# A planned attention and two gated MLPs on one core: planner costs from a trace, the words' guard offered to GpSimd, later weights let in at set points

## The chip, the cores and the metric

The kernel runs on one core of a Trainium2 chip. The metric is the device time of one execution in microseconds (us). The kernel before took 1058.9 us (median of 3 runs, 1057.39 to 1060.78).

## The reference

```python
# attention: 4 batches, 8 heads, 576 positions, 64 columns a head, all float32
scores = where(mask, scale * q @ k.T, -1e9)     # heads 0-3: a window of 32; heads 4-7: 32 steps of 4 back
attn   = softmax(scores);  o = attn @ v
x = o laid out as 2304 tokens x 512
# first gated MLP, d_ff 1536
xn = x / sqrt(mean(x * x) + 1e-6) * rms_g
x  = (silu(xn @ w_gate) * (xn @ w_val)) @ w_out
# second gated MLP, d_ff 1536
y  = (sigmoid(x @ w_gate2) * (x @ w_val2)) @ w_out2
```

The MLP weights arrive in 8-byte floating point and are read as pairs of 32-bit words.

## The kernel before

**Products.** Every operand of an MLP product is split into a high and a low part (`split`: the high part is a cast on ScalarE, the low part a subtraction on GpSimd; VectorE may do either), and a product is three matmuls: high by high, high by low, low by high.

**Stages.** Attention works in 48 groups of three blocks of 64 queries (`attn_group`): scores on TensorE (L709), mask and row maximum on VectorE (L720), exponential on ScalarE (L726), the sum's reciprocal on VectorE (L733, L734), normalisation on GpSimd (L739), transposes on TensorE (L751), values on TensorE (L763). When the groups of a chunk of 384 tokens are done, `x_norm` makes that chunk's operand: squares on ScalarE (L807), sums on GpSimd (L815) and TensorE (L823), a Newton iteration (twelve small GpSimd operations, L857 to L861), a copy `rb` on VectorE (L864), its transposes on TensorE (L879), a scaling on VectorE (L891, tile `xn`, two buffers) and a split into `xo`. The transposes of `rb`, the scores and the transposes of the groups share a ring of two PSUM banks, `att`.

The first MLP runs in two passes over d_ff, each with 6 chunks of tokens by 6 blocks of 128 rows of d_ff: 72 steps. A step is a gate product `g`, a value product `v` (both L982) and an output product `y` (L1019), 12 matmuls each for g, v and y; between them stand tanh on ScalarE (L994), two multiplications on VectorE (L996, L1000) and the split of `h`. The steps of the first pass begin while attention still runs, and the groups stand between them on TensorE. The second MLP has three passes; its gate and value products are block products with fewer multiplications (`unit`, L1160), whose sums are added on VectorE (L1176), gated (L1186, L1192) and split into `h`. It needs sums and differences of the weights (L496 on VectorE, L499 on GpSimd) and of its input (L935, L938).

**Weights.** `words` turns the 64-bit weights into float32: a square on ScalarE (L395), a guard on VectorE that zeroes what is too small (L401, one input, 128 x 512), and three VectorE operations that put the bits together (L404, L407, L410, two inputs each). The 18 weight tiles of the first pass are split at once; the 18 of the second pass and the 36 of the second MLP are stored to HBM and loaded again when they are due.

**Order.** The whole order is written by a planner (`Line.emit`). Every operation is added with its engines, a cost in us, a due time and its reads and writes. The planner keeps a clock for each engine, picks the operation that can start first, and emits it; so the costs and due times decide the order in which instructions stand in each engine's queue. An operation with `other=` may go to a second engine; a number of `PARAMS` is added to that engine's start as a penalty. `release` holds an operation back until the planner's clock has come so far. On the chip each engine runs its queue in order and waits for semaphores.

Of the kernel before, what the change touches and what calls it, by code (L numbers as in the profile page):

```python
# [8 lines left out]
F32 = mybir.dt.float32  # L9
F32R = mybir.dt.float32r  # L10
# [16 lines left out]
    "h_hi": 0.3, "h_lo": 0.5, "qk": 0.2, "norm": 4.0, "pts": 4.0, "o": 2.0, "snap": 150.0, "h_ahead": 50.0, "h2_ahead": 50.0, "evac": 150.0, "ys": 1.0,  # L27
    "ts": 1.0, "cross": 0.25, "same": 0.064, "dma_lat": 2.0, "dma_rate": 260e3,
# [171 lines left out]
def attention_then_two_gated_mlps(  # L200
# [26 lines left out]
    ONE, TWO = 2, 3  # L227
    NF1 = DF // P // ONE
# [138 lines left out]
    def words(p, f, i, load_due, due, release=0.0):  # L367
# [22 lines left out]
        def low():  # L390
# [79 lines left out]
    def weight_load(p, f, i, due):  # L470
        key = (layer_of(p), f, i)
        z = new("mid", "zm", [P, CW], F32, 3 * NF1) if p == 1 else one_of(Z_HOMES, [P, CW], F32)
# [4 lines left out]
    def weight_late(p, f, i, due):  # L477
        z = weight_load(p, f, i, due - 6 - 40 * (p == 1))
# [180 lines left out]
    def attn_load(b, hp, due):  # L659
# [33 lines left out]
    def attn_group(b, hp, g, due, banks, start):  # L693
# [55 lines left out]
        def turn():  # L749
# [50 lines left out]
    def x_norm(c, due, banks):  # L800
# [226 lines left out]
    def y_first(p, c, m, due):  # L1027
# [21 lines left out]
        if m < KD - 1:  # L1049
            return  # L1050
# [365 lines left out]
```

## Time and profile before

| | |
|---|---|
| median of three runs | 1058.9 us |
| the profiled execution: its own time | 1064.26 us |
| the profiled execution: its span | 1062.3 us |
| TensorE busy | 1001.8 us (94%) |
| VectorE, ScalarE, GpSimd busy | 692.7, 461.1, 524.4 us |
| HBM read, written | 103.55, 47.19 MB |

The span goes from the first to the last instruction; the execution's own time is 2.0 us more. Busy time says how long an engine had an instruction under way, blocked time in the instruction included, and not whether the end depended on it. PE is TensorE, DVE VectorE, ACT ScalarE, POOL GpSimd.

### The profile page before, as it was taken

The page shows a single profiled execution, that of the slowest core. Times are in us where ns is not written, and L with a number is a line of the kernel's source. Part 1 is how long each engine was busy: PE and PEld are TensorE (multiplying, and loading weights), DVE is VectorE, ACT ScalarE, POOL GpSimd, SP SyncE. Part 2 cuts the span into 40 slices and gives each one's busy share as a digit, 9 for nine tenths or more (in the row PEclk, how much of TensorE's full clock was granted, in tenths as well). Part 3 has the DMA queues.
Part 4 walks back from the last instruction along what each step waited for, and adds up shares of the span by engine and source line. Part 5 has one row for each costly group of instructions (what it writes and reads, how often), then busy time and mean ns, then how long its engine had stood idle before and what let it go on. Part 6 is the DMA issues. An engine that isn't in the chain of part 4 may idle for free.

```text
span 1062.3 us, 19957 instructions
## 1 busy us (share of the span) xinstructions
PE 1001.8 (94%) x7222; PEld 966.2 (91%) x7222; DVE 692.7 (65%) x1443; ACT 461.1 (43%) x1251; POOL 524.4 (49%) x671
## 2 busy tenths in 40 slices
PE   4978869999999999999999999999999999999997
PEld 3767758888899999999999989999999999999996
DVE  2689787876664697766656575658556675465633
ACT  2967545655532443222222354445554354444321
POOL 2557765555552585112223683538655385444411
PEclk7769879999999999999999999999999998999999
DMA  9648746867349466765672331204231333235234
GB/s 189 130 112 182 171 134 156 206 154 223 106 150 346 158 219 212 275 221 179 199 248 72 97 114 45 89 24 131 81 137 63 134 110 107 97 100 125 54 82 90
DMA packets 192978, 152.04 MB, mean 143 GB/s; under 512 B 135760, under 2 KB 164432, under 8 KB 192880
## 3 DMA queue, kind: packets, MB, share of 16 engines
q1 hardware_dynamic: 185896, 149.00, 47.8%
q10 hardware_dynamic: 6984, 1.77, 1.0%
q8 instruction: 57, 0.93, 0.4%
q14 instruction: 41, 0.34, 0.1%
HBM read 103.55 MB, written 47.19 MB: 142 GB/s over the span
## 4 chain that ended last, share of the span: by engine, by line
PE 75%; DVE 9%; DMA 5%; POOL 3%; issue 3%; ACT 3%; SPq 2%; ACTq 0%; DVEq 0%; POOLq 0%
PE y L1019 23%; PE g L982 12%; PE v L982 11%; PE att L1160 10%; PE g L1160 7%; PE v L1160 7%; PE att L709 2%; DVE wz L401 1%; ACT pr L726 1%; DMA wst<-in_moe_w_val_dram 1%; POOL pr L739 1%; DMA v<-in_v_dram 1%; DVE wz L404 1%; PE att L763 1%; SPq L621 1%
## 5 line engine op out<-in xcount | busy, mean ns | idle before, releaser
L1019 PE MATMUL y<-h,wo 128*128 128x288 f32 (+1 forms) x2016 | 371.6, 314 | 1.1 <-POOL h L421 1.1
L1019 PEld LDWEIGHTS y<-h,wo 128*128 128x128 f32 x2016 | 319.5, 189 | 3.7 <-POOL h L421 1.3
L421 POOL TENSOR_TENSOR h<-t,h 128x288 fp32r<-128x288 f32 (+1 forms) x157 | 160.4, 1024 | 282.5 <-ACT h L417 231.4
L982 PE MATMUL g<-xo,w 128*128 128x384 f32 x864 | 169.1, 344 | 4.1 <-ACT w L417 1.7
L982 PE MATMUL v<-xo,w 128*128 128x384 f32 x864 | 163.5, 337 | 0.0
L982 PEld LDWEIGHTS g<-xo,w 128*128 128x128 f32 x864 | 154.7, 193 | 6.3 <-ACT w L417 1.9
L982 PEld LDWEIGHTS v<-xo,w 128*128 128x128 f32 x864 | 150.1, 188 | 1.3 <-issue 0.2
L417 ACT CAST h<-t 128x288 fp32r<-128x288 f32 (+1 forms) x144 | 67.3, 471 | 151.8 <-DVE t L1000 99.8
L1176 DVE TENSOR_TENSOR t<-t,att 128x288 f32<-128x288 f32 x96 | 43.1, 449 | 79.0 <-PE att L1160 78.5
L994 ACT ACTIVATE t<-g 128x384 f32<-128x384 f32 x72 | 35.4, 492 | 132.4 <-PE g L982 132.3
L1160 PE MATMUL att<-xo,w 128*128 128x288 f32 x576 | 92.5, 296 | 0.0
L739 POOL TENSOR_SCALAR pr<-pr,rs 128x96 f32<-128x96 f32 x144 | 63.4, 456 | 49.2 <-DVE rs L734 29.4
L996 DVE SCALAR_TENSOR_TENSOR t<-t,g 128x384 f32<-128x384 f32 x72 | 39.7, 551 | 73.2 <-ACT t L994 73.0
L1160 PEld LDWEIGHTS att<-xo,w 128*128 128x128 f32 x576 | 82.0, 189 | 0.0
L421 POOL TENSOR_TENSOR xo<-xq,xo 128x576 fp32r<-128x576 f32 x35 | 52.8, 1516 | 35.2 <-ACT xo L417 32.8
L1160 PE MATMUL v<-xo,w 128*128 128x288 f32 x396 | 64.6, 299 | 3.1 <-DVE t L1176 2.9
L401 DVE TENSOR_SCALAR wz<-wz 128x512 f32<-128x512 f32 x72 | 48.7, 678 | 27.1 <-ACT wz L395 25.7
L1160 PE MATMUL g<-xo,w 128*128 128x288 f32 x396 | 64.7, 300 | 0.0
L407 DVE SCALAR_TENSOR_TENSOR wz<-wst,wz 128x512 int32<-128x512 int32 x72 | 63.2, 877 | 1.0
L410 DVE SCALAR_TENSOR_TENSOR wz<-wst,wz 128x512 int32<-128x512 int32 x72 | 61.3, 853 | 1.2
L404 DVE SCALAR_TENSOR_TENSOR wz<-wst,wz 128x512 int32<-128x512 int32 x72 | 60.8, 845 | 1.1
L726 ACT ACTIVATE pr<-pr,nmx 128x96 f32<-128x96 f32 x144 | 52.5, 369 | 18.8 <-DVE nmx L720 18.6
(166 smaller groups left out, 1587.7 us busy)
## 6 DMA issues: line engine op xcount, KB each, us to landing
z<-wz SPq DMA_DIRECT2D x54, 256.0 KB, 2.2
wst<-in_moe_w_gate_dram SPq DMA_DIRECT2D x24, 512.0 KB, 3.9
wst<-in_moe_w_val_dram SPq DMA_DIRECT2D x24, 512.0 KB, 5.7
wst<-in_moe_w_out_dram SPq DMA_DIRECT2D x24, 512.0 KB, 4.2
xq<-y SPq DMA_DIRECT2D x20, 576.0 KB, 5.4
x<-xo SPq DMA_DIRECT2D x12, 768.0 KB, 4.7
xo<-x SPq DMA_DIRECT2D x12, 768.0 KB, 6.3
z<-z SPq DMA_DIRECT2D x36, 256.0 KB, 2.8
```

What stands on the lines that cost most here:

```text
L401: add("DVE", 0.65, lambda: nc.vector.tensor_scalar(out=z.t.bitcast(F32), in0=z.t.bitcast(F32), scalar1=LEAST * LEAST, scalar2=MANTISSA, op ...
L404: add("DVE", 0.9, lambda: nc.vector.scalar_tensor_tensor(out=z.t, in0=top(), scalar=3, in1=z.t, op0=ALU.logical_shift_left, op1=ALU.bitwis ...
L407: add("DVE", 0.9, lambda: nc.vector.scalar_tensor_tensor(out=z.t, in0=top(), scalar=-0x40000000, in1=z.t, op0=ALU.bitwise_and, op1=ALU.bit ...
L410: add("DVE", 0.9, lambda: nc.vector.scalar_tensor_tensor(out=z.t, in0=low(), scalar=29, in1=z.t, op0=ALU.logical_shift_right, op1=ALU.bitw ...
L417: add("ACT", act(n), lambda: nc.scalar.copy(out=hi(), in_=src()), reads=reads, writes=[key] + [order] * bool(order), tiles=tiles + [dst], ...
L421: add("PL", pool(n), lambda: nc.gpsimd.tensor_tensor(out=lo(), in0=src(), in1=hi().bitcast(F32), op=ALU.subtract), reads=reads, writes=[ke ...
L726: add("ACT", PARAMS["exp_cost"], lambda u=u: nc.scalar.activation(out=pr.t[:, u], in_=pr.t[:, u], func=ACTF.Exp, bias=nmx.t[:, u:u + 1], s ...
L739: add("PL", 0.33, lambda u=u: nc.gpsimd.tensor_scalar(out=pr.t[:, u], in0=pr.t[:, u], scalar1=rs.t[:, u:u + 1], scalar2=1.0, op0=ALU.mult, ...
L982: nc.tensor.matmul(out=bank.t, lhsT=w[:, l, cols], rhs=x[:, r, j], start=kk == 0 and n == 0, stop=kk == KD - 1 and n == 2)
L1019: nc.tensor.matmul(out=yb.t, lhsT=w.t[:, l, s], rhs=h.t[:, r], start=n == 0 and j == 0, stop=n == nf - 1 and j == 2)
L1160: nc.tensor.matmul(out=bank.t, lhsT=l.t[:, a, cols], rhs=r.t[:, d, j], start=first and j == 0 and m == 0, stop=j == 1 and m == 2, skip_gro ...
L1176: add("DVE", dve(T), lambda: nc.vector.tensor_tensor(out=t.t, in0=t.t, in1=bank.t, op=ALU.add), reads=[(key, uk)], writes=[ck[name]], tile ...
```

## The change

Four things change.

1. The planner's costs in attention and in `x_norm` are raised: mask 0.224 to 0.335, exponential 0.387 to 0.56, reciprocal 0.3 to 0.43, normalisation 0.33 to 0.47, the copy `pts` 0.37 to 0.48, the VectorE transposes 0.67 to 0.95, the Newton parts 1.95 to 2.6 and others.
2. The guard of `words` may go to GpSimd, with a cost of 1.3 against VectorE's 0.65 and no penalty.
3. The words of the second pass are let in from the planner's time 180 on (before: 57 + 1.2 t, from about 117), and those of the second MLP from 360 over 190 (before: from 290 over 250).
4. Penalties and due times: `o` 2.0 to 0.3, `ts` 1.0 to 0.2, `snap` 150 to 200, `lo5` 80 to 95.

The passes of the first MLP are also written for any partition of d_ff (`holds`); with (6, 6) they are the two passes of before.

```diff
@@ PARAMS
-    "o": 2.0, "snap": 150.0,
+    "o": 0.3, "snap": 200, "holds": (6, 6), "guard": 0.0, "recip": 0.43,
+    "rel1": 180, "span1": 60.0, "rel2": 360.0, "span2": 190.0,
-    "ts": 1.0,
+    "ts": 0.2,
-    "hi4": 108.9, "lo5": 80.0,
+    "hi4": 108.9, "lo5": 95,
-    "mask_cost": 0.224, "exp_cost": 0.387, "s_cost": 0.8,
-    "t_cost": 0.36,
+    "mask_cost": 0.335, "exp_cost": 0.56, "s_cost": 0.75,
+    "t_cost": 0.38,
@@ words
-        add("DVE", 0.65, lambda: nc.vector.tensor_scalar(
-            out=z.t.bitcast(F32), in0=z.t.bitcast(F32), scalar1=LEAST * LEAST, scalar2=MANTISSA,
-            op0=ALU.is_ge, op1=ALU.mult), writes=[zk], tiles=[z], due=due)
+        def guard(eng):
+            eng.tensor_scalar(
+                out=z.t.bitcast(F32), in0=z.t.bitcast(F32), scalar1=LEAST * LEAST,
+                scalar2=MANTISSA, op0=ALU.is_ge, op1=ALU.mult)
+
+        add("DVE", 0.65, lambda: guard(nc.vector), writes=[zk], tiles=[z], due=due,
+            other=("guard", "PL", 1.3, lambda: guard(nc.gpsimd)))
@@ attn_group
-        add("DVE", 0.3, recip, reads=[("e", gk, u) for u in range(G)], writes=[("rs", gk)],
+        add("DVE", PARAMS["recip"], recip, reads=[("e", gk, u) for u in range(G)], writes=[("rs", gk)],
-            add("PL", 0.33, lambda u=u: nc.gpsimd.tensor_scalar(
+            add("PL", 0.47, lambda u=u: nc.gpsimd.tensor_scalar(
-        add("ACT", 0.37, lambda: nc.scalar.copy(out=pts.t, in_=pt.t), reads=[("pt", gk)],
+        add("ACT", 0.48, lambda: nc.scalar.copy(out=pts.t, in_=pt.t), reads=[("pt", gk)],
@@ x_norm
-            add("PL", 1.95, newton_aside, writes=[yk], tiles=[a, y, ms], due=due)
+            add("PL", 2.6, newton_aside, writes=[yk], tiles=[a, y, ms], due=due)
@@ whole
-        for n in range(3 * NF1):
-            f, i = divmod(n, 3)
-            t = (8 + 24 * n / (3 * NF1)) * STEP
-            weight_ahead(1, NF1 + f, i, t - 8, t, 57 + 1.2 * t)
+        later = [(p, f, i) for p in range(1, ONE) for f in range(HOLDS[p]) for i in range(3)]
+        for n, (p, f, i) in enumerate(later):
+            use = (NC1 * FIRST[p] + f + (1.66 if i == 2 else i * 0.33)) * STEP
+            weight_ahead(p, FIRST[p] + f, i, use - 40, use - 32,
+                         PARAMS["rel1"] + PARAMS["span1"] * n / len(later))
-            weight_ahead(p, f, i, t - 8, t, 290 + 250 * n / len(todo))
+            weight_ahead(p, f, i, t - 8, t, PARAMS["rel2"] + PARAMS["span2"] * n / len(todo))
```

What this does to the queues is seen in the order of the instructions. Lines of the changed kernel have other numbers: L716 scores, L758 group transposes, L770 values, L886 the transposes of `rb`, L989 g and v, L1026 y; L405 the guard, L746 the normalisation, L428 and L431 the low parts, L822 the sums; L942 the differences of the second MLP's input, L1190 the sums of its products, L1206 its gating.

TensorE's queue at the norm of the second chunk (the fifth step of the first pass), the kernel before:

```order
L709 MATMUL att<-kT,qT 64x96 x6
L982 MATMUL v<-xo,w 128x384 x12
L1019 MATMUL y_1229<-h,wo 128x384 x3
L1019 MATMUL y_1236<-h,wo 128x384 x3
L1019 MATMUL y_1255<-h,wo 128x384 x3
L1019 MATMUL y_1264<-h,wo 128x384 x3
L879 MATMUL att<-ident,rb 128x128 x3
L751 MATMUL att<-ident,pr 96x128 x6
L982 MATMUL g<-xo,w 128x384 x12
L763 MATMUL att<-pts,v 64x64 x12
```

And the changed kernel at the same place:

```order
L989 MATMUL g<-xo,w 128x384 x12
L886 MATMUL att<-ident,rb 128x128 x3
L989 MATMUL v<-xo,w 128x384 x12
L1026 MATMUL y_1198<-h,wo 128x384 x3
L1026 MATMUL y_1205<-h,wo 128x384 x3
L1026 MATMUL y_1232<-h,wo 128x384 x3
L1026 MATMUL y_1242<-h,wo 128x384 x3
L770 MATMUL att<-pts,v 64x64 x6
L758 MATMUL att<-ident,pr 96x128 x6
L770 MATMUL att<-pts,v 64x64 x6
L989 MATMUL g<-xo,w 128x384 x12
```

The transposes of `rb` stood between a y product and two groups' transposes; now a g product stands ahead of them, and a v product, a y product and a group's values stand between them and the next groups' transposes.

GpSimd's queue shortly ahead of that norm, the kernel before:

```order
L421 TENSOR_TENSOR w<-wz,w 128x256 x4
L739 TENSOR_SCALAR pr<-pr,rs 128x96 x3
L421 TENSOR_TENSOR h<-t,h 128x384
L421 TENSOR_TENSOR wo<-wz,wo 128x512
L739 TENSOR_SCALAR pr<-pr,rs 128x96 x3
L815 TENSOR_TENSOR pt<-pt 128x384
L421 TENSOR_TENSOR w<-wz,w 128x256
L815 TENSOR_TENSOR pt<-pt 128x384
L421 TENSOR_TENSOR w<-wz,w 128x256
L815 TENSOR_TENSOR pt<-pt 128x384
L421 TENSOR_TENSOR w<-wz,w 128x256 x2
L739 TENSOR_SCALAR pr<-pr,rs 128x96 x3
```

And the changed kernel:

```order
L428 TENSOR_TENSOR w<-wz,w 128x256 x2
L746 TENSOR_SCALAR pr<-pr,rs 128x96 x3
L405 TENSOR_SCALAR wz<-wz 128x512
L746 TENSOR_SCALAR pr<-pr,rs 128x96 x3
L428 TENSOR_TENSOR wo<-wz,wo 128x512
L428 TENSOR_TENSOR h<-t,h 128x384
L405 TENSOR_SCALAR wz<-wz 128x512
L428 TENSOR_TENSOR w<-wz,w 128x256 x2
L657 MEMSET v 32x128
L746 TENSOR_SCALAR pr<-pr,rs 128x96
L822 TENSOR_TENSOR pt<-pt 128x384
L405 TENSOR_SCALAR wz<-wz 128x512
```

Three guards stand between the normalisations and splits that were there before. Over the whole program 50 of the 72 guards are on GpSimd, 13 of them among the first 18 words (steps 0 to 5), and VectorE keeps 22.

VectorE's queue in the first unit of the second MLP, the kernel before (T and `xq` are differences of the input of the next token block, `t<-t,v` the sum that the seventh value product waits for):

```order
L419 CAST xo_7278<-xq 128x576
L1176 TENSOR_TENSOR t_7280<-t_7280,att 128x288
L1192 SCALAR_TENSOR_TENSOR t_7232<-t_7232,t_7280 128x288
L935 TENSOR_TENSOR T_7305<-xq 128x576
L935 TENSOR_TENSOR xq<-xq 128x576
L1176 TENSOR_TENSOR t<-t,v 128x288
L935 TENSOR_TENSOR xq<-xq 128x576
L1192 SCALAR_TENSOR_TENSOR t_7256<-t_7256,t 128x288
L935 TENSOR_TENSOR xq<-xq 128x576
L1176 TENSOR_TENSOR t_7300<-t_7300,att 128x288
```

And the changed kernel:

```order
L426 CAST w_7253<-S 128x256
L431 TENSOR_TENSOR w_7253<-S,w_7253 128x256
L1190 TENSOR_TENSOR t_7251<-t_7251,att 128x288
L1206 SCALAR_TENSOR_TENSOR t_7211<-t_7211,t_7251 128x288
L426 CAST h<-t_7211 128x288
L1190 TENSOR_TENSOR t<-t,v 128x288
L1206 SCALAR_TENSOR_TENSOR t_7222<-t_7222,t 128x288
L1190 TENSOR_TENSOR t_7274<-t_7274,att 128x288
```

Two of the four differences stood ahead of the sum `t<-t,v`; now they come after it, and a cast of `h` stands there.

## Rows read from the trace of the kernel before

**Rows 1.** Four stretches: length, busy PE, PEld, DVE, ACT, POOL; clock, DMA, GB/s.
```profile
67.80:150.00 82.20, 64.39 (x510) 54.38 (x509) 69.30 (x180) 50.38 (x164) 62.71 (x96) 0.83 0.68 169
150.00:300.00 150.00, 145.50 (x1243) 131.77 (x1243) 110.51 (x328) 83.25 (x278) 80.15 (x156) 1.00 0.65 171
300.00:614.00 314.00, 313.42 (x1818) 313.00 (x1815) 208.78 (x317) 98.77 (x209) 131.51 (x128) 1.00 0.58 194
614.00:665.00 51.00, 46.11 (x320) 44.81 (x319) 34.21 (x53) 23.20 (x54) 28.41 (x24) 0.97 0.25 78
```

**Rows 2.** Timeline of PE, 133 to 153 us: start, us, what, idle before.
```profile
133.02 0.52 PE L879 MATMUL att<-ident,rb 128*128 128x128 f32 x3 [1.76 <-DVE rb L864]
141.26 0.85 PE L751 MATMUL att<-ident,pr 128*96 128x128 f32 x3 [7.72 <-DVE xn L891]
143.40 0.88 PE L751 MATMUL att<-ident,pr 128*96 128x128 f32 x3 [1.29 <-DVE nmx L720]
143.93 4.04 PE L982 MATMUL g<-xo,w 128*128 128x384 f32 x12
...
150.96 2.24 PE L1019 MATMUL y<-h,wo 128*128 128x384 f32 x12
```

**Rows 3.** Timeline of DVE, 132 to 142 us.
```profile
132.32 0.55 DVE L864 COPY rb<-rsy 128x384 f32<-128x384 f32 x1 [2.58 <-POOL rsy L861]
...
140.38 0.73 DVE L891 SCALAR_TENSOR_TENSOR xn<-xT,gam,att 128x192 f32<-128x192 f32 x2
```

**Rows 4.** Groups by line and shape: busy us, mean ns, idle before.
```profile
L739 POOL TENSOR_SCALAR pr<-pr,rs 128x96 f32<-128x96 f32 x144 | 63.4, 456 | 49.2 <-DVE rs L734 29.4 <-DVE nmx L720 12.2 <-ACT pr L726 3.3
...
L401 DVE TENSOR_SCALAR wz<-wz 128x512 f32<-128x512 f32 x72 | 48.7, 678 | 27.1 <-ACT wz L395 25.7 <-DMA kraw<-in_k_dram 1.3
...
L421 POOL TENSOR_TENSOR wo<-wz,wo 128x512 fp32r<-128x512 f32 x6 | 8.1, 1349 | 3.7 <-ACT wo L417 3.7
...
L859 POOL TENSOR_SCALAR rsa<-rsa 128x3 f32<-128x3 f32 x15 | 3.7, 247 | 1.4
```

**Rows 5.** Instructions of L401 and of L739: ns min/median/max.
```profile
L401 DVE TENSOR_SCALAR wz<-wz x72: 396/428/3808, 19.1 to 566.3; 128x512 f32<-128x512 f32 x72
...
L739 POOL TENSOR_SCALAR pr<-pr,rs x144: 335/347/1288, 28.0 to 295.7; 128x96 f32<-128x96 f32 x144
```

**Rows 6.** Timeline of POOL, 101 to 128 us.
```profile
101.36 2.98 POOL L739 TENSOR_SCALAR pr<-pr,rs 128x96 f32<-128x96 f32 x3 [0.43 <-DVE rs L734]
...
127.35 0.98 POOL L739 TENSOR_SCALAR pr<-pr,rs 128x96 f32<-128x96 f32 x3
```

**Rows 7.** Timeline of PE ahead of the first step.
```profile
59.45 0.83 PE L823 MATMUL v<-ones,pt 128*128 128x1 f32 x6
64.31 0.90 PE L879 MATMUL y<-ident,rb 128*128 128x128 f32 x3 [4.04 <-DVE rb L864]
...
65.78 1.22 PE L709 MATMUL att<-kT,qT 64*64 64x96 f32 x12
66.94 0.91 PE L763 MATMUL att<-pts,v 96*64 96x64 f32 x12
```

**Rows 8.** Timeline of PE at the change between the MLPs, and later.
```profile
618.00 2.17 PE L1019 MATMUL y<-h,wo 128*128 128x384 f32 x11 [1.08 <-POOL h L421]
...
632.26 1.06 PE L1160 MATMUL v<-wst,w 128*128 128x288 f32 x6 [1.46 <-DVE t L1176]
...
646.14 1.81 PE L1160 MATMUL v<-wst,w 128*128 128x288 f32 x6 [2.32 <-DVE t L1176]
...
878.75 1.81 PE L1160 MATMUL v<-xo,w 128*128 128x288 f32 x6 [2.94 <-DVE t L1176]
```

**Rows 9.** Chain that ended last, at the same places: start, us, what.
```profile
628.66 1.93 DVE T L935
...
642.73 1.44 DVE h L419
...
876.76 1.20 DVE xq L935
```

More of the change, by code (lines that the diff above doesn't have):

```diff
@@ L226, in attention_then_two_gated_mlps @@
     KD = DM // P
-    ONE, TWO = 2, 3
-    NF1 = DF // P // ONE
+    HOLDS = PARAMS["holds"]
+    ONE, TWO = len(HOLDS), 3
+    FIRST = [sum(HOLDS[:p]) for p in range(ONE + 1)]
+    assert FIRST[-1] == DF // P
     NF = DF // P // TWO
@@ L471, in weight_load @@
         key = (layer_of(p), f, i)
[L472 removed]
+        z = new("mid", "zm", [P, CW], F32, 18) if p < ONE else one_of(Z_HOMES, [P, CW], F32)
         dma(lambda: nc.sync.dma_start(out=z.t, in_=z_scr[key]), 262e3,
@@ L867, in x_norm @@
         if c:
-            add("DVE", 0.55, seed, reads=[("ssp", c)], writes=[yk], tiles=[ssp, ms, a, y], due=due)
-            add("PL", 1.95, newton_aside, writes=[yk], tiles=[a, y, ms], due=due)
-            add("DVE", 0.47, spread, reads=[yk], writes=[("rb", c)], tiles=[y, rb], due=due)
+            add("DVE", 0.75, seed, reads=[("ssp", c)], writes=[yk], tiles=[ssp, ms, a, y], due=due)
+            add("PL", 2.6, newton_aside, writes=[yk], tiles=[a, y, ms], due=due)
+            add("DVE", 0.56, spread, reads=[yk], writes=[("rb", c)], tiles=[y, rb], due=due)
         else:
-            add("DVE", 2.9, lambda: (seed(), newton(), spread()), reads=[("ssp", c)],
+            add("DVE", 3.7, lambda: (seed(), newton(), spread()), reads=[("ssp", c)],
                 writes=[("rb", c)], tiles=[ssp, ms, a, y, rb], due=due)
@@ L905, in attention_then_two_gated_mlps, with x_load @@
     NX = 4
-    def x_load(c, due):
-        xo = xtile[1, c] = [new("sb", "xo", [P, 2, 2, T1], F32R, NX) for _ in range(2)]
+    def x_load(p, c, due):
+        xo = xtile[p, c] = [new("sb", "xo", [P, 2, 2, T1], F32R, NX) for _ in range(2)]
         for k in range(2):
@@ L911, in x_load @@
                 out=xo[k].t.bitcast(F32), in_=x_scr[2 * c + k].bitcast(F32)), 786e3,
-                reads=[("scr", c, k)], writes=[("xo", 1, c, 2 * k + j) for j in range(2)] +
+                reads=[("scr", c, k)], writes=[("xo", p, c, 2 * k + j) for j in range(2)] +
                 ["x order"], tiles=[xo[k]], due=due)
@@ L1040, in y_first @@
             if m == KD - 1:
-                dma(lambda: nc.sync.dma_start(out=y_part[c], in_=ys.t), 786e3,
-                    reads=[("sum", 0, c, i) for i in range(KD)], writes=[("part", 0, c)],
-                    tiles=[ys], due=due)
+                part_store(p, c, due)
             return
@@ L1049, in y_first @@
         if m < KD - 1:
+            return
+        if p < ONE - 1:
+            part_store(p, c, due)
             return
@@ L1059, in y_first, with part_store @@
             done += n
+    def part_store(p, c, due):
+        t = parts[p, c]
+        dma(lambda: nc.sync.dma_start(out=y_part[c], in_=t.t), 786e3,
+            reads=[("sum", p, c, i) for i in range(KD)], writes=[("part", p, c)], tiles=[t],
+            due=due)
     def part_load(p, c, due):
@@ L1063, in part_load @@
             return
-        if p == 1:
+        if p < ONE:
             t = parts[p, c] = new("sb", "pt", [P, KD, T1], F32, 2)
             dma(lambda: nc.sync.dma_start(out=t.t, in_=y_part[c]), 786e3,
-                reads=[("part", 0, c), ("bank", p, c, p * NF1, 0)],
+                reads=[("part", p - 1, c), ("bank", p, c, FIRST[p], 0)],
                 writes=[("sum", p, c, m) for m in range(KD)] + ["pt order"], tiles=[t], due=due)
@@ L1248, in whole @@
             span = span[len(due):]
-            lo, hi = PARAMS[f"lo{c}"], PARAMS[f"hi{c}"]
+            lo, hi = (PARAMS[f"{i}{c}"] * HOLDS[0] / 6 for i in ("lo", "hi"))
             for i, g in enumerate(span):
@@ L1294, in whole @@
             [("xo", 0, c, kk) for c in range(NC1) for kk in range(KD)])
-        for n in range(3 * NF1):
+        for n in range(3 * HOLDS[0]):
             f, i = divmod(n, 3)
@@ L1318, in whole @@
             for c in range(NC1):
-                for fi in range(NF1):
-                    s = (NF1 * (NC1 * p + c) + fi) * STEP
+                for fi in range(HOLDS[p]):
+                    s = (NC1 * FIRST[p] + HOLDS[p] * c + fi) * STEP
                     if p and not fi:
-                        x_load(c, s - 25)
-                    mlp_step(p, c, p * NF1 + fi, s)
+                        x_load(p, c, s - 25)
+                    mlp_step(p, c, FIRST[p] + fi, s)
                     if prev:
```

32 lines of the change are left out of this document (16 added, 16 removed), and 2 rows, old and new, of the table PARAMS.

## The prediction

> **What bounds the kernel now.** I read the busy times by stretch first, then the timelines of TensorE, VectorE and GpSimd where TensorE is not full, then the groups by line. The stretches show that there is little left to win in most of the span [rows 1]: TensorE is busy for 313.42 of 314.00 us between 300 and 614 us, and for 145.50 of 150.00 us ahead of that. It has room in two places. From 67.8 us, where the first MLP step starts, to 150 us it is busy for 64.39 of 82.20 us, so 17.8 us idle, and its granted clock is 0.83 on the mean. From 614 to 665 us, where the second MLP starts, it is idle for 4.9 of 51.0 us at 0.97. In the first of these VectorE is busy for 69.30 and GpSimd for 62.71 of 82.2 us: these two bound that stretch, by their work or by the order of it.
>
> The largest hole is at the norm of the second chunk [rows 2]: 1.76 us in front of the transposes of `rb`, 7.72 us in front of a group's transposes, 1.29 us in front of the next group's, 10.8 us together. The middle one was released by the scaling L891: the transposes of `rb` fill a bank of the ring `att`, the scaling reads it until 141.1 us, and the group's transposes need it. VectorE writes `rb` from 132.32 us and the last scaling starts at 140.38 us [rows 3], because words stand between the scalings in its queue. [...]
>
> **The change part by part.** The sum is made against the profiled execution, 1064.26 us (span 1062.3 us and 2.0 us around it). That is 5.4 us above the median of 1058.9 us, so I carry the difference over to the median.
>
> *The norm of the second chunk.* In the changed queue of TensorE a g product (2.24 us) now stands ahead of the transposes of `rb`, and a v product, a y product (2.24 us each) and a group's values (0.6 us, two thirds of the 0.91 us at the lower clock in [rows 7]) stand between them and the next transposes. That is work that is only moved, so each us of it that falls into a wait is won. The wait of 1.76 us goes (-1.5, the g product being longer than it). For the second wait I count VectorE's new queue from `rb` to the last scaling: `rb` 0.55, five word operations at about 0.68 and a guard at 0.43, three masks with their reads at 0.25, a reciprocal pair 0.34, a low part 0.65, two gate multiplications 0.54 each, and eight scalings 2.84, some 10 us, against the 8.8 us of before (132.32 to 140.38 + 0.73). With 5.1 us of product work under it, about 4.9 us of the 7.72 are left: -2.8. If that transpose draws the other bank, all 7.72 go; if GpSimd is late with the splits (`xn` has two buffers), none. The third wait goes, since its masks now stand ahead of the scalings: -1.3. With a shorter hole I expect about 1.1 us of the 1.8 us that the lower clock costs the g product back. Together -6.7; bounds 0 and -12.6 (10.8 + 1.8).
>
> *The guards on GpSimd.* 13 of the first 18 guards move. No row shows a GpSimd operation with one input of 512 columns. From above: L859 has 3 columns at 247 ns and L739 96 at 456 ns, 2.25 ns a column, 1.39 us at 512 [rows 4]. From below: with L739's median of 347 ns [rows 5] it is 1.08 ns a column, 0.80 us. I take 1.35 us, the mean of the split `wo`, which has the same 512 columns [rows 4]. VectorE loses the guard's 0.68 us on the mean, 0.43 us where nothing disturbs it [rows 4, 5]. So GpSimd gets 13 x 1.35 = 17.6 us, which just fits into its 19.5 us of idle time between 67.8 and 150 us [rows 1], and VectorE loses 13 x 0.68 = 8.8 us. Each of these words now crosses from ScalarE to GpSimd to VectorE, and VectorE's queue stands at L404 until GpSimd has come to the guard; masks and scalings queue behind it, and TensorE waits for those. What hides this is the slack that VectorE wins. The net work of both engines lies between 13 x (0.80 - 0.68) = +1.6 us and 13 x (1.39 - 0.43) = +12.5 us; if none of it reaches the path, 0. I take a little under half the net of my two values (17.6 - 8.8 = 8.8): +4.
>
> The trace shows that these two engines do not run beside each other freely: three normalisations take 0.98 us at one time and 2.98 us at another [rows 6], and the guard, 428 ns in the median, has taken 3.81 us [rows 5]. [...]
>
> *Words of later passes.* In steps 6 to 10 the changed queues hold no guard where there were five, so VectorE is freed of five words there; but from 150 to 300 us TensorE has only 4.5 us of idle time in all [rows 1]. I take -0.5, bounds 0 and -4.5. These words come back later, in the stretch from 300 to 614 us, six of them in the last nine steps instead of two. TensorE's 0.6 us of idle time there [rows 1] says that it does not wait for them; the cover is that a step's work is done by engines that are at most two thirds busy. If the cover goes, the splits of the second MLP's first weights come late; that is in the next term.
>
> *Start of the second MLP.* The last split of `h` is wholly on VectorE now and no longer behind a split of `xo` on GpSimd: the wait of 1.08 us goes. The wait of 1.46 us in front of the seventh value product was made by a difference of 1.93 us ahead of the sum `t` [rows 8, 9]; it is now behind it, and a short cast stands there: -1.4. The wait of 2.32 us was made by a cast of 1.44 us and its low part [rows 8, 9], which have moved behind too, but three sums of weights have come ahead: -1, and with it 0.5 us of lower clock. Against this stand four more words in the last steps and weight splits that stand later in GpSimd's queue: +1. Together -3, bounds -6.4 (all three waits and 1.5 us of clock) and +4 (four words at about 3.3 us on VectorE, a third of it uncovered).
>
> *Later in the second MLP.* TensorE's queue is nearly the same. At 878.75 us it waits 2.94 us for a sum that stood behind a difference of 1.20 us [rows 8, 9]; GpSimd has that difference now: -1.2. The seven other differences that GpSimd gets lie beside a full TensorE: bounds -3 and +2.
>
> *Ahead of the first step.* The transposes of the first chunk's `rb` waited 4.04 us; a group's scores and values (1.22 and 0.91 us) now stand ahead of them [rows 7]. The raised costs may also push the masks and reciprocals of the first twelve groups either way: -1.5, bounds -4 and +3.
>
> Sum: -6.7 + 4 - 0.5 - 3 - 1.2 - 1.5 = -8.9, so 1055.4 us for a profiled execution and 1050 us for the median.
>
> **The rivals.**
> *GpSimd becomes the bound of the first chunk* (slower). The 17.6 us do not fit, since its 19.5 us of idle time are themselves waits for ScalarE and VectorE, and most of the 62.71 us is blocked or needed [rows 1, 6]. The guards then delay the first weights by their net, +12.5, VectorE stands at L404, and the splits of `xo` come late, so the queue at the norm gains only its first wait (-1.5). With -3 in the second MLP this is +8: 1067 us. It decides once GpSimd has under some 3 us of idle time in steps 1 to 5. The trace's swings of normalisation and guard speak for it; against it, VectorE gets rid of the operation that blocks and is blocked. [...]
>
> *All the holes close.* The costs fit, and the whole 17.8 us of idle time up to 150 us, less 4 us that remain at the two norms, goes together with the second MLP's 4: -18, 1041 us. For it: words and scalings no longer alternate on VectorE. Against it: work of both engines is 132 of 164 us already.
>
> *Nothing that counts.* The chunk's products keep the same place among the groups (after 24 groups TensorE's queue has 5.5 steps before, 6 now), and what the norm gains the guards take; or the plan's better costs do not bear on the chip's order at all. 1059 us.
>
> **How the numbers follow.** Forecast (1044 to 1055): 0.45. All holes close (under 1044): 0.10. Nothing that counts (within 3.2 us, which is 0.3% and about what a measurement of this kernel tells from no change): 0.17. GpSimd bound (over 1062): 0.28. Faster is the first two, 0.55; same 0.17; slower 0.28. The range goes from 1040 to 1067: it leaves out a little under a tenth below (half of the second case and the far end of the forecast's bounds) and a little over a tenth above, where the first rival's price is exceeded because the second MLP's gain fails as well. The forecast's own range is 1044 to 1055.
>
> **What would show it.** Right: the three waits around the second chunk's transposes of `rb` add up to about 5 us instead of 10.8, the stretch from the first step to the sixth is 4 us or more shorter, no wait of over 1 us in front of the last y product, and the waits near 632 and 879 us smaller. The guard on GpSimd shows a mean between 0.8 and 1.4 us. Wrong: new waits of TensorE in steps 1 to 5 that end on GpSimd's guard or on L404 behind it, GpSimd busy over 95% there, or weights that the first units of the second MLP wait for.

## The result: slower, and the guard's length is why

The changed kernel took 1070.3 us (median of 6 runs, 1068.32 to 1073.15), the kernel before 1059.0 us beside it (6 runs, 1056.48 to 1062.65): ratio 1.0105, 95% interval 1.0079 to 1.0131. The forecast was 1050 us with 1040 to 1067. The profiled execution took 1071.6 us, its span 1069.8 us.

The page of the changed kernel, as far as it answers to [rows 4]: busy time and share of each engine; the shares of the chain that ended last; then groups (busy us, mean ns of one, idle before it and what ended most of it).

```profile
PE 1008.3 (94%) x7222; PEld 967.6 (90%) x7222; DVE 672.0 (63%) x1398; ACT 461.2 (43%) x1248; POOL 626.9 (59%) x719
...
PE 75%; POOL 10%; DVE 6%; issue 3%; DMA 3%; ACT 3%; SPq 0%; DVEq 0%; POOLq 0%; ACTq 0%
...
L989 PE MATMUL g<-xo,w 128*128 128x384 f32 x864 | 170.8, 345 | 9.7 <-POOL w L428 5.0
L989 PE MATMUL v<-xo,w 128*128 128x384 f32 x864 | 165.6, 339 | 5.5 <-POOL w L428 4.5
...
L405 POOL TENSOR_SCALAR wz<-wz 128x512 f32<-128x512 f32 x50 | 103.6, 2072 | 64.4 <-ACT wz L398 58.3
...
L411 DVE SCALAR_TENSOR_TENSOR wz<-wst,wz 128x512 int32<-128x512 int32 x72 | 54.2, 752 | 50.5 <-POOL wz L405 49.9
```

The same shares of the chain in the kernel before:

```profile
PE 75%; DVE 9%; DMA 5%; POOL 3%; issue 3%; ACT 3%; SPq 2%; ACTq 0%; DVEq 0%; POOLq 0%
```

GpSimd's share of the chain went from 3% to 10%. 50 of the 72 guards run on GpSimd and take 103.6 us there, 2.07 us each on the mean. VectorE, which goes on with L411 behind the guard, waits 49.9 us for them. The operation itself, in the instructions of that line (min/median/max), beside VectorE's own guards:

```profile
L405 POOL TENSOR_SCALAR wz<-wz x50: 1921/1931/2457, 19.6 to 598.9; 128x512 f32<-128x512 f32 x50
...
L405 DVE TENSOR_SCALAR wz<-wz x22: 398/775/1242, 58.0 to 604.2; 128x512 f32<-128x512 f32 x22
```

So a guard takes 1.93 us on GpSimd when nothing disturbs it. The prediction took 1.35 us and had bounded it by 0.80 and 1.39.

The four stretches, in the columns of [rows 1]:

```profile
67.80:150.00 82.20, 65.03 (x529) 53.39 (x530) 59.26 (x177) 48.72 (x170) 75.66 (x98) 0.87 0.60 142
150.00:300.00 150.00, 146.87 (x1216) 132.31 (x1215) 92.18 (x297) 81.04 (x265) 94.21 (x166) 0.98 0.60 154
300.00:614.00 314.00, 309.45 (x1781) 307.20 (x1780) 206.07 (x300) 96.87 (x203) 177.20 (x143) 0.99 0.60 205
614.00:665.00 51.00, 45.83 (x298) 44.70 (x297) 39.49 (x57) 26.23 (x62) 40.92 (x38) 0.97 0.31 96
```

In the first stretch GpSimd went from 62.71 to 75.66 us and VectorE from 69.30 to 59.26. TensorE, which had 0.58 us of idle time between 300 and 614 us, now has 4.55 us there.

TensorE's waits in the changed kernel, where they answer to [rows 2] and [rows 8]:

```profile
109.08 3.45 PE L989 MATMUL g<-xo,w 128*128 128x384 f32 x10 [2.22 <-POOL w L428]
124.37 0.91 PE L770 MATMUL att<-pts,v 96*64 96x64 f32 x12 [2.04 <-DVE nmx L727]
134.73 1.32 PE L989 MATMUL v<-xo,w 128*128 128x384 f32 x6 [2.53 <-POOL w L428]
149.50 3.00 PE L989 MATMUL g<-xo,w 128*128 128x384 f32 x10 [2.50 <-POOL w L428]
158.63 0.50 PE L758 MATMUL att<-ident,pr 128*96 128x128 f32 x3 [0.55 <-DVE xn L898]
...
628.56 2.18 PE L1026 MATMUL y<-h,wo 128*128 128x384 f32 x11 [0.73 <-DVE h L431]
634.71 1.06 PE L1174 MATMUL g<-wst,w 128*128 128x288 f32 x6 [0.78 <-ACT t L1184]
648.84 1.05 PE L1174 MATMUL g<-wst,w 128*128 128x288 f32 x6 [0.90 <-DVE t L1190]
657.47 1.06 PE L1174 MATMUL v<-wst,w 128*128 128x288 f32 x6 [2.76 <-DVE t L1190]
...
888.95 1.07 PE L1174 MATMUL v<-xo,w 128*128 128x288 f32 x6 [1.49 <-DVE t L1190]
```

The hole of 7.72 us at the second chunk's norm is gone (0.55 us there), and so is half of the one near 879 us. In their place TensorE waits for weights' low parts (`w`, L428), three times here and 9.5 us in all by the two groups of g and v above, where the kernel before waited 1.1 us for them; GpSimd makes them after the guards that it now has. The guards are not the whole of these waits: with the same order and all guards on VectorE they are still 5.9 us (e9 below). VectorE's wait for such a guard, on GpSimd and then on VectorE:

```profile
130.03 1.93 POOL L405 TENSOR_SCALAR wz<-wz 128x512 f32<-128x512 f32 x1
```
```profile
132.00 0.69 DVE L411 SCALAR_TENSOR_TENSOR wz<-wst,wz 128x512 int32<-128x512 int32 x1 [2.57 <-POOL wz L405]
```

Later guards cost as well. The chain that ended last, near 326 us (start, us, what):

```profile
320.43 1.94 POOL wz L405
...
322.39 0.70 DVE wz L411
...
323.11 1.39 DVE wz L414
324.50 1.05 DVE xn L898 x2
...
330.19 1.84 POOL xo L428 x2
...
333.08 1.45 POOL h L428
...
334.57 3.71 PE y L1026 x11
```

Two operations of GpSimd's own queue at this place (start, us):

```profile
322.43 1.52 POOL L428 TENSOR_TENSOR h<-t,h 128x384 fp32r<-128x384 f32 x1
...
328.18 1.93 POOL L405 TENSOR_SCALAR wz<-wz 128x512 f32<-128x512 f32 x1
```

The guard at 320.43 us holds back VectorE's word, the word holds back the scalings of the next operand, and their split on GpSimd holds back the split of `h`; a second guard, from 328.18 us, stands ahead of the last two of these splits (`xo`, from 330.19 us). The y product then waits 2.32 us and takes 3.71 us for 11 matmuls (2.24 us for 12 shortly before); the granted clock from 320 to 345 us is 0.93. With the same order and the guards on VectorE (e1) the same product waits 0.34 us:

```profile
315.32 2.18 PE L1026 MATMUL y<-h,wo 128*128 128x384 f32 x11 [0.34 <-POOL h L428]
```

By the first g matmul of a step in both timelines, the 26th step starts 4.3 us later than in the kernel before, the 27th 9.7 us.

### The profile page after: what moved, and what is told of

Its sections match the earlier page's. It is cut to its first block, busy times and chain, and to the rows that moved or that the text cites. A ratio compares the mean times of both kernels' runs of the same rounds, so it can differ in the third digit from the quotient of the medians.

```text
span 1069.8 us, 19886 instructions
## 1 busy us (share of the span) xinstructions
PE 1008.3 (94%) x7222; PEld 967.6 (90%) x7222; DVE 672.0 (63%) x1398; ACT 461.2 (43%) x1248; POOL 626.9 (59%) x719
## 4 chain that ended last, share of the span: by engine, by line
PE 75%; POOL 10%; DVE 6%; issue 3%; DMA 3%; ACT 3%; SPq 0%; DVEq 0%; POOLq 0%; ACTq 0%
PE y L1026 25%; PE g L989 11%; PE v L989 10%; PE att L1174 10%; PE g L1174 7%; PE v L1174 7%; POOL wz L405 3%; PE att L716 2%; POOL pr L746 2%; POOL w L428 1%; DMA xT<-in_v_dram 1%; PE att L770 1%; PE att L758 1%; POOL xo L428 1%; POOL h L428 1%
## 5 line engine op out<-in xcount | busy, mean ns | idle before, releaser
L1026 PE MATMUL y<-h,wo 128*128 128x288 f32 (+1 forms) x2016 | 375.0, 316 | 3.7 <-POOL h L428 3.0
L1026 PEld LDWEIGHTS y<-h,wo 128*128 128x128 f32 x2016 | 323.8, 190 | 6.1 <-POOL h L428 3.9
L428 POOL TENSOR_TENSOR h<-t,h 128x288 fp32r<-128x288 f32 (+1 forms) x149 | 149.3, 1005 | 190.7 <-ACT h L424 152.9
L989 PE MATMUL g<-xo,w 128*128 128x384 f32 x864 | 170.8, 345 | 9.7 <-POOL w L428 5.0
L989 PE MATMUL v<-xo,w 128*128 128x384 f32 x864 | 165.6, 339 | 5.5 <-POOL w L428 4.5
L989 PEld LDWEIGHTS g<-xo,w 128*128 128x128 f32 x864 | 153.5, 192 | 14.6 <-POOL w L428 6.1
L989 PEld LDWEIGHTS v<-xo,w 128*128 128x128 f32 x864 | 150.7, 189 | 7.9 <-POOL w L428 5.5
L405 POOL TENSOR_SCALAR wz<-wz 128x512 f32<-128x512 f32 x50 | 103.6, 2072 | 64.4 <-ACT wz L398 58.3
L1190 DVE TENSOR_TENSOR t<-t,att 128x288 f32<-128x288 f32 x96 | 43.1, 449 | 73.0 <-PE att L1174 72.2
L411 DVE SCALAR_TENSOR_TENSOR wz<-wst,wz 128x512 int32<-128x512 int32 x72 | 54.2, 752 | 50.5 <-POOL wz L405 49.9
L1174 PEld LDWEIGHTS att<-xo,w 128*128 128x128 f32 x576 | 82.2, 189 | 0.0
L746 POOL TENSOR_SCALAR pr<-pr,rs 128x96 f32<-128x96 f32 x144 | 61.2, 439 | 25.5 <-DVE rs L741 15.8
L414 DVE SCALAR_TENSOR_TENSOR wz<-wst,wz 128x512 int32<-128x512 int32 x72 | 66.6, 925 | 1.2
L1007 DVE TENSOR_TENSOR t<-t,v 128x384 f32<-128x384 f32 x72 | 39.7, 551 | 37.9 <-PE v L989 37.5
L428 POOL TENSOR_TENSOR xo<-xq,xo 128x576 fp32r<-128x576 f32 x35 | 54.0, 1553 | 15.6 <-ACT xo L424 15.5
```

The costliest lines, as they stand in the source:

```text
L405: eng.tensor_scalar(out=z.t.bitcast(F32), in0=z.t.bitcast(F32), scalar1=LEAST * LEAST, scalar2=MANTISSA, op0=ALU.is_ge, op1=ALU.mult)
L411: add("DVE", 0.9, lambda: nc.vector.scalar_tensor_tensor(out=z.t, in0=top(), scalar=3, in1=z.t, op0=ALU.logical_shift_left, op1=ALU.bitwis ...
L414: add("DVE", 0.9, lambda: nc.vector.scalar_tensor_tensor(out=z.t, in0=top(), scalar=-0x40000000, in1=z.t, op0=ALU.bitwise_and, op1=ALU.bit ...
L428: add("PL", pool(n), lambda: nc.gpsimd.tensor_tensor(out=lo(), in0=src(), in1=hi().bitcast(F32), op=ALU.subtract), reads=reads, writes=[ke ...
L746: add("PL", 0.47, lambda u=u: nc.gpsimd.tensor_scalar(out=pr.t[:, u], in0=pr.t[:, u], scalar1=rs.t[:, u:u + 1], scalar2=1.0, op0=ALU.mult, ...
L989: nc.tensor.matmul(out=bank.t, lhsT=w[:, l, cols], rhs=x[:, r, j], start=kk == 0 and n == 0, stop=kk == KD - 1 and n == 2)
```

## The experiments

Most of them keep the changed kernel's plan to the last place in each queue and change only where or how the guard is executed; so the order is no part of the difference.

**e1 and e9: the same plan, the guard on VectorE.**

```diff
-            other=("guard", "PL", 1.3, lambda: guard(nc.gpsimd)))
+            other=("guard", "PL", 1.3, lambda: guard(nc.vector)))
```

> The changed kernel's plan, kept to the last place in every queue, but each guard that the plan gives to GpSimd is issued on VectorE at its place in the order. Theory A (a guard takes 1.93 us or more on GpSimd, where I had taken 1.35, and VectorE stands at L411 meanwhile): 50 guards leave GpSimd (some 100 us of its busy time) and VectorE gets 50 x 0.43 to 0.78 us; the steps 2 to 6 lose the 9.7 us that they had gained, the hole at 326 us goes, and the time is 1054 to 1062 us. Theory B (the plan's raised costs, its due times and the later words cost the time, wherever the guard runs): 1068 to 1073 us, as the changed kernel. L411's wait for a guard on GpSimd (49.9 us) is gone in both.

1046.8 us (4 runs, 1043.5 to 1051.7), ratio to before 0.9888 (0.9854 to 0.9921). That is 23.5 us under the changed kernel and below what even theory A had expected: in this order the rest of the change gains. The run was repeated:

> The changed kernel's plan with all guards issued on VectorE, a second time, since it is faster than both kernels. It was 1046.8 us in four executions (1043.5 to 1051.7). If that is the kernel's time: 1045 to 1050 us, ratio to before 0.986 to 0.992. If those four were a draw of the start (the first step began at 61.9 us there, at 69.2 us in another kernel with the same instructions up to that point): 1050 to 1054 us, and the ratio 0.992 to 0.996.

1048.8 us (6 runs, 1047.5 to 1051.2), ratio 0.9918 (0.9896 to 0.9940). Of the versions timed in several runs this is the fastest, and faster than both kernels. Its first two stretches, and TensorE's waits at the norm and near 865 us:

```profile
67.80:150.00 82.20, 69.47 (x579) 61.02 (x578) 67.17 (x192) 52.24 (x179) 64.70 (x102) 0.87 0.61 151
150.00:300.00 150.00, 149.14 (x1244) 135.97 (x1243) 96.98 (x306) 80.82 (x263) 79.56 (x153) 1.00 0.63 167
```
```profile
135.39 3.57 PE L989 MATMUL g<-xo,w 128*128 128x384 f32 x10 [3.37 <-POOL w L428]
145.08 0.51 PE L758 MATMUL att<-ident,pr 128*96 128x128 f32 x3 [0.53 <-DVE xn L898]
...
865.05 1.06 PE L1174 MATMUL v<-xo,w 128*128 128x288 f32 x6 [1.51 <-DVE t L1190]
```

TensorE is busy for 69.47 us of the first stretch instead of 64.39 [rows 1]. Its waits for weights' low parts ahead of g products (us in all, times, longest):

```profile
PE g L989 <- POOL w L428: 5.6, 2, 3.4
```

With 0.3 us ahead of a v product that makes 5.9 us, against 9.5 us in the changed kernel. Between the first step and the 14th TensorE is idle for 20.6 us in the kernel before, 18.9 us in the changed kernel and 13.5 us in e9.

**e5 and e6: the guards of the first pass or of the later passes alone on GpSimd.**

```diff
+            other=("guard", "PL", 1.3, lambda: guard(nc.vector if p else nc.gpsimd)))   # e5
+            other=("guard", "PL", 1.3, lambda: guard(nc.gpsimd if p else nc.vector)))   # e6
```

> The changed kernel's plan, each instruction at its place; only the first pass's guards stand on GpSimd where the plan put them, those of later passes are issued on VectorE. Between the changed kernel and the run with the same plan and all guards on VectorE the step starts differ by 13.8 us at the sixth step, 15.6 at step 15 and 23.1 at the last. Theory A (most of the loss is the first chunk's, where GpSimd has no room): 1060 to 1064 us. Rival (the 32 or more later guards cost as much or more): 1048 to 1057 us.

> The reverse of the run before: the first pass's guards on VectorE, those of later passes on GpSimd where the plan put them. Theory A: 1047 + 5 to 9 us, 1052 to 1056 us, from the hole near 326 us and those of the last steps, with the first six steps as in the run with all guards on VectorE. Rival (later guards carry most): 1060 us or more. If the two runs' losses add up to 23.5 us, the parts do not hide each other.

e5 took 1057.7 us (10 runs; ratio 0.9998, 0.9982 to 1.0014), e6 1060.3 us (10 runs; 1.0009, 0.9987 to 1.0032). Against e9 that is +9.0 us for 13 guards of the first pass and +11.5 us for 37 later ones, together 20.5 of the 21.5 us between the changed kernel and e9. From the first step to the end of the span, in the profiled executions, it is +7.6 and +8.5 of 18.7 us. My theory had put most of the loss into the first chunk; the later guards carry as much or a little more.

**e7: a shorter guard on GpSimd.**

```diff
-            other=("guard", "PL", 1.3, lambda: guard(nc.gpsimd)))
+            other=("guard", "PL", 1.3, lambda: guard(nc.gpsimd, 128)))   # 128 of 512 columns
```

> The changed kernel; where the guard stands on GpSimd it covers 128 of the 512 columns only (so the other columns' words are not those of the reference). Crossings ScalarE to GpSimd to VectorE, and every place in a queue, stay as in the changed kernel; only the guard's length on GpSimd falls, by 3.77 ns a column to some 0.5 us. If its length is the cause: 1046 to 1054 us, and L411's wait for it falls from 49.9 us to under 20. If the crossing is (VectorE's queue stands until GpSimd comes to the guard, whatever it takes): 1062 to 1071 us.

1053.2 us (6 runs, 1048.2 to 1056.3; ratio 0.9942, 0.9917 to 0.9967), and 0.65 us a guard:

```profile
L405 POOL TENSOR_SCALAR wz<-wz x50: 641/648/1102, 19.6 to 585.0; 128x128 f32<-128x128 f32 x50
```

VectorE still waits 22.3 us for it, a little more than I had expected, and from the first step to the end the profiled execution takes 984.8 us, as long as e9's (984.9): the crossing itself costs nothing there. Its median is 4.4 us above e9's; the profiled execution has that, and more, ahead of its first step (69.7 against 60.9 us; see the last section).

**e11 to e14: what makes the guard dear.** The guard's two operations on GpSimd, comparison and multiplication, were replaced by others over the same 512 columns.

```diff
-                scalar2=MANTISSA, op0=ALU.is_ge, op1=ALU.mult)
+                scalar2=MANTISSA, op0=ALU.mult, op1=ALU.mult)     # e11, on GpSimd
+                scalar2=MANTISSA, op0=ALU.mult, op1=ALU.min)      # e12, with scalar1=2.0 ** 31
+                scalar2=MANTISSA, op0=ALU.mult, op1=ALU.add)      # e13
+                scalar2=None, op0=ALU.is_ge)                      # e14
```

> The changed kernel with the guard's comparison on GpSimd replaced by a multiplication (two multiplications over the same 512 columns, so the words made there are not those of the reference). The normalisation, two multiplications over 96 columns, takes 347 ns in the median, the guard over 128 columns 648 ns and over 512 columns 1931 ns. If the comparison is what makes the guard dear: 0.8 to 1.4 us each, as I had bounded it. If it is the width, 3.3 ns a column: 1.93 us again.

> The changed kernel with the guard on GpSimd written as a multiplication by 2 to the 31 and a minimum with the mask (zero stays zero, every ordinary weight gives the mask; only weights under about 2 to the -127 that are not zero would come out otherwise, and there are none). Two multiplications took 618 ns over 512 columns, a comparison and a multiplication 1931 ns. If it is the step from a multiplication to any operation that compares, the minimum costs as much as the comparison: 1.5 to 2.0 us a guard and 1062 to 1072 us. If it is the comparison that yields 0 or 1 alone: 0.62 us a guard and 1046 to 1052 us, which would be a form in which the guard does fit on GpSimd.

> The changed kernel with the guard on GpSimd as a multiplication and an addition (the words made there are not those of the reference). Two multiplications took 618 ns over 512 columns; comparison and multiplication 1931 ns, multiplication and minimum 1923 ns. If an operation that compares is what triples the time: about 0.62 us a guard and 1045 to 1053 us. If it is that the two operations are not alike: 1.9 us and 1062 to 1073 us.

> The changed kernel with the guard on GpSimd as the comparison alone, without a second operation (the words made there are not those of the reference). If the comparison is dear by itself: 1.9 us and 1062 to 1073 us. If it is the pair of unlike operations: 0.6 us or less and 1045 to 1053 us.

The guard's instructions on GpSimd in e11, e12, e13 and e14 (min/median/max; L410 is e12's line of it):

```profile
L405 POOL TENSOR_SCALAR wz<-wz x50: 617/618/1062, 19.5 to 577.3; 128x512 f32<-128x512 f32 x50
```
```profile
L410 POOL TENSOR_SCALAR wz<-wz x50: 1919/1923/2457, 19.2 to 593.3; 128x512 f32<-128x512 f32 x50
```
```profile
L405 POOL TENSOR_SCALAR wz<-wz x50: 617/620/1087, 19.3 to 575.3; 128x512 f32<-128x512 f32 x50
```
```profile
L405 POOL TENSOR_SCALAR wz<-wz x50: 1488/1502/1969, 19.1 to 586.4; 128x512 f32<-128x512 f32 x50
```

Two arithmetic operations take 0.62 us, alike or not; a comparison alone takes 1.50 us, and a comparison or a minimum with a multiplication 1.92 to 1.93 us. So it is the operation that compares, by the two that were tried, is_ge and min; the 1.50 us of the comparison alone lie between the two values that I had expected. (In e13 the addition yields the mask for every ordinary weight; what it leaves out is only the zeroing of the smallest, less than its expectation says.) The time follows it, in one and the same plan:

| guards that the plan gives to GpSimd | us of one | time, us | first step to end of the span, us |
|---|---|---|---|
| issued on VectorE (e9) | 0.43 | 1048.8 (6 runs) | 984.9 |
| two multiplications (e11) | 0.62 | 1048.8 (1 run) | 986.5 |
| multiplication, addition (e13) | 0.62 | 1046.8 (1 run) | 984.3 |
| comparison, 128 columns (e7) | 0.65 | 1053.2 (6 runs) | 984.8 |
| comparison alone (e14) | 1.50 | 1058.8 (1 run) | 995.6 |
| multiplication, minimum (e12) | 1.92 | 1065.9 (4 runs) | 1001.2 |
| comparison, multiplication (changed kernel) | 1.93 | 1070.3 (6 runs) | 1003.6 |

Up to 0.65 us a guard on GpSimd is hidden, to within 2 us in all; from there to 1.93 us the 50 guards cost 19 us (last column). The 0.43 us of the first row are the median here:

```profile
L405 DVE TENSOR_SCALAR wz<-wz x72: 396/427/1646, 19.7 to 580.6; 128x512 f32<-128x512 f32 x72
```

Why a comparison alone takes longer than two multiplications (1502 against 618 ns in the median), the runs do not show.

**e3, e4, e2, e8 and e10: other plans.**

```diff
 # e3: the kernel before, and in words the offer alone
+            other=("guard", "PL", 1.3, lambda: guard(nc.gpsimd)))
 # e8: as e3, the guards that the plan gives GpSimd issued on VectorE
+            other=("guard", "PL", 1.3, lambda: guard(nc.vector)))
 # e4: the changed kernel
-            other=("guard", "PL", 1.3, lambda: guard(nc.gpsimd)))
+            other=("guard", "PL", 1.95, lambda: guard(nc.gpsimd)))
 # e2: the changed kernel;  e10: as e2, and VectorE's words at 0.45 and 0.7 instead of 0.65 and 0.9
-    "guard": 0.0
+    "guard": 1e4
```

> The kernel before with one part of the change alone: the guard may go to GpSimd, at the plan's cost of 1.3 and without a penalty. Theory A: slower than before by the guards' net in the first chunk, 13 or more guards x (1.95 - 0.68) us, less what hides: 1065 to 1076 us, with VectorE's waits for the guard of 30 us or more. Theory B: no change, 1056 to 1062 us.

1068.2 us (4 runs; ratio 1.0083, 1.0067 to 1.0098): the offer alone makes the kernel before slower by 9.5 us.

> The changed kernel with the guard's cost on GpSimd in the plan at 1.95 us, as its trace shows, instead of 1.3. If the plan's wrong price is the cause (it puts guards where GpSimd has no time for them), the plan now gives GpSimd only those that fit: 1052 to 1060 us. [...] By theory B: 1068 to 1073 us.

1065.4 us (4 runs; 1.0062, 1.0041 to 1.0083). With the true length as its price the plan still gives GpSimd 53 guards, so the wrong price was not what put them there; that the plan sees room on GpSimd's clock where the chip's queues have none is my reading, and no run tests it.

> The changed kernel with a penalty of 10,000 on the guard's second engine, so that the plan itself keeps all guards on VectorE; all other parts of the change stand. Theory A with the other terms of the prediction (-6.7 for the norm of the second chunk, -3 and -1.2 in the second MLP, -1.5 ahead of the first step, -0.5): 1046 to 1052 us. Theory A with the rest worth nothing: 1057 to 1061 us. Theory B (the rest of the change is what costs): 1066 us or more.

1057.2 us (10 runs; 0.9986, 0.9968 to 1.0005): with this order the rest of the change is worth nothing that counts. This is 8.4 us above e9, which has its guards on VectorE as well and differs in the order, and in the engine of the few other operations that a plan may place.

> The kernel before with the offer alone in the plan (price 1.3 on GpSimd), as in the run with that part alone, but the guards that the plan gives GpSimd are issued on VectorE at their places. The run with the changed kernel's plan and VectorE's guards took 1046.8 us, the one whose plan knows of no offer 1057.2. If the gain of some 10 us comes from how a plan with the offer orders the words, whatever its other prices: 1046 to 1052 us. If it needs the changed prices of the attention and the later words as well: 1055 to 1060 us.

1057.9 us (10 runs; 1.0000, 0.9987 to 1.0014): the offer's plan with the old prices gains nothing.

> The changed kernel without the offer to GpSimd, with VectorE's words at the price that the trace shows when nothing disturbs them (guard 0.45 instead of 0.65, the three bit operations 0.7 instead of 0.9). Three plans with all guards on VectorE took 1057.2, 1057.9 and 1046.8 us; the last one had put 50 guards on GpSimd's clock and so saw VectorE freer than it was. If that view of VectorE is what made the order better: 1045 to 1052 us. If the fast order is one draw among many: 1053 to 1062 us.

1050.9 us (6 runs; 0.9930, 0.9908 to 0.9952). A plan that sees VectorE's words at their true length is nearly as good as the plan that saw 50 guards elsewhere. That speaks for the view of VectorE as the cause of e9's better order, but two plans do not show it: what in e9's order is better than in e2's was not taken apart.

## Why the prediction was wrong

The step that failed is the term for the guards, "+4", and in it the length: "I take 1.35 us", between 0.80 and 1.39. Both bounds came from operations of GpSimd that only multiply, add or subtract. The guard, which compares, takes 1.93 us. The 37 guards of later passes had no term at all. Two sentences fell with it: that 13 guards "just fit" into 19.5 us of idle time (13 x 1.93 = 25.1 us), and that the net work is at most +12.5.

Point by point, from the profiled executions, by the start of the first g matmul of a step and the first matmul of a unit against the kernel before. The middle column is e1 or e9, the same queues with the guard on VectorE:

| term | forecast | guards on VectorE | changed kernel |
|---|---|---|---|
| ahead of the first step | -1.5 | -5.8 (e1), -6.8 (e9) | -1.6 |
| first to 14th step: norm of the second chunk and words of later passes (changed kernel: with 13 guards, +4) | -6.7 - 0.5 | -5.1 (e9) | +3.2 |
| 14th to last step | 0 | -0.8 (e9) | +9.6 |
| last step to fourth unit of the second MLP | -3 | +0.8 (e1) | +0.8 |
| fourth unit to the end of the span | -1.2 | -4.5 (e1) | -4.5 |

The profiled execution of the kernel before was 5.4 us above that kernel's median, e9's 1.1 us below its own. So e9's differences add up to -16.4 us where its median is 8.5 us below that of the kernel before, and the changed kernel's to +7.5 us where its median is 11.3 us above: several us against the kernel before can belong to the execution. Differences between e9 and the changed kernel are freer of this.

*Norm of the second chunk: right in mechanism.* The wait of 7.72 us for the scaling went, more of it than the 2.8 us I had counted, and without the guards the first 13 steps gain 5.1 us where the two terms said 7.2; what I had not foreseen are the waits for weights' low parts (1.1 us before, 5.9 us in e9). The 2.8 us were also a wrong sum: VectorE's queue being 1.2 us longer and 5.1 us of products standing under it, 3.8 us of the 7.72 would have been left, not 4.9. No run shows by itself the 1.1 us that the term expects back from a lower clock; what the traces show is a granted clock of 0.54 from 143.9 to 148 us, at the g product behind the hole [rows 2], and in the changed kernel 1.00 at the g product behind that norm (2.35 us, from 160.48 us) but 0.62 at the one ahead of it (3.00 us for 10 matmuls, from 149.50 us).

*Guards: wrong in size and in place.* From the first to the last step the changed kernel loses 12.8 us and e9 gains 5.9: 18.7 us against my +4. Not quite half of it (8.3 us) falls up to the 14th step. The other half belongs to the 37 guards of later passes, which I had costed at nothing because "a step's work is done by engines that are at most two thirds busy". The share was true (GpSimd 177.20 of 314 us), but the chain near 326 us shows that it does not protect: with one guard of 1.94 us ahead of a norm's scalings and one ahead of their splits, TensorE waits 2.32 us there instead of 0.34 (and 2.30 us in e6, with the later guards alone on GpSimd).

*Ahead of the first step: cannot be told.* e6 has e9's queues up to the first step, and its profiled execution began that step 8.2 us later; the term lies within such draws.

*Start of the second MLP: wrong by 4 us.* The three waits became four (0.73, 0.78, 0.90 and 2.76 us, 5.2 together against 4.86), since other sums of products are late now. No run shows the 0.5 us of clock in this term: the granted clock from 614 to 665 us is 0.97 in both kernels. *Later:* the wait of 2.94 us became 1.49, as said; the stretch from 870 to 920 us also has a granted clock of 1.00 instead of 0.93, which the forecast had left out. This gain belongs to the change and not to one execution: the changed kernel and all twelve runs made from it show -4.4 to -4.6 us in this row, the two made from the kernel before -0.2 (e3) and -1.4 (e8).

So the sum without its guard term, -12.9 us or 1046 us, was met by the two runs with the guards on VectorE, 1046.8 and 1048.8 us. Part of that is luck: the start of the second MLP came out 3.8 us worse than its term and the rest of it 3.3 us better. And part is luck of the order: e2, a plan without the offer, has the same other changes and gains 1.6 us, which its interval does not tell from nothing.

*The first rival* was right in sign and near in time (1067 us). GpSimd was busy for 75.66 of 82.2 us in the first stretch, 92% and not over 95%, and its mechanism held for half the loss only. *Beside each other.* The swings in [rows 5] and [rows 6] left open whether one of the two engines stands for the whole of the other's operation. The changed kernel's trace shows less than that. Two of VectorE's word operations beside one guard of the changed kernel, first VectorE's queue, then GpSimd's:

```profile
436.57 0.68 DVE L414 SCALAR_TENSOR_TENSOR wz<-wst,wz 128x512 int32<-128x512 int32 x1
...
437.64 0.69 DVE L417 SCALAR_TENSOR_TENSOR wz<-wst,wz 128x512 int32<-128x512 int32 x1
```
```profile
436.75 2.29 POOL L405 TENSOR_SCALAR wz<-wz 128x512 f32<-128x512 f32 x1 [1.28 <-ACT wz L398]
...
439.12 1.52 POOL L428 TENSOR_TENSOR h<-t,h 128x384 fp32r<-128x384 f32 x1
```

VectorE's two operations take 0.68 and 0.69 us here, their medians over the 72 words being 696 and 692 ns, and the guard is 0.36 us longer than its median: neither waits for a whole instruction of the other. Beside GpSimd's subtraction L428 the same L414 takes 1.39 us (at 439.80 us and, near 326 us, at 323.11 us). The two engines do slow each other, then: a guard takes up to 2.46 us, and the mean is 0.14 us above the median of 1.93. But most of what the guards cost is their own length and who waits for them, not a stand for a whole instruction.

## What to carry to other kernels

Bound an operation that no row shows by rows with the same arithmetic on that engine, not only the same shape: on GpSimd a comparison took 2.4 times as long as two multiplications over the same columns. Before work moves to an engine that is half idle, follow who waits for each piece: here a guard of 1.94 us ahead of a norm's scalings, and one of 1.93 us ahead of their splits, made TensorE wait 2.32 us instead of 0.34. To tell an order from an engine, keep the plan and swap only the engine of one operation; the two can have opposite signs, as here.

## What was not expected of the hardware

Besides the comparison on GpSimd: the stretch ahead of the first step differs from execution to execution. e1 and e6 have the same queues up to their first step; here is the stretch from 30 to 40 us and the first g matmul of e1, then of e6:

```profile
30.00:40.00 10.00, 8.60 (x144) 6.98 (x140) 7.86 (x43) 8.69 (x41) 5.48 (x19) 1.00 0.67 101
```
```profile
61.95 0.69 PE L989 MATMUL g<-xo,w 128*128 128x384 f32 x1 [1.25 <-ACT xo L424]
```
```profile
30.00:40.00 10.00, 10.00 (x99) 7.84 (x98) 3.63 (x24) 6.47 (x29) 3.08 (x10) 0.50 0.67 94
```
```profile
69.18 0.69 PE L989 MATMUL g<-xo,w 128*128 128x384 f32 x1 [1.25 <-ACT xo L424]
```

The granted clock is 1.00 in one and 0.50 in the other; 144 matmuls run in those 10 us, or 99, and the first step starts 7.2 us apart. The two ran on different chips, but the chip alone does not make the difference: e5, on e6's chip and with queues that differ up to there only in the engine of the guards, begins its first step at 61.95 us as e1 does. The cause stays open. Two profiles of this kernel are therefore best compared from their first step on, and times by medians.
